# Head sums by ScalarE's accumulator, value blocks added up in PSUM, batch 0 in quarters and joined tails, in a linear-attention and gated-unit kernel

## The chip, the cores and the metric

The kernel runs on one core of one Trainium2 chip. The metric is the device time of one execution in microseconds (us). A core has five engines with a queue of instructions each: TensorE (PE, its weight loads shown apart as PEld), VectorE (DVE), ScalarE (ACT), GpSimd (POOL) and SyncE (SP), which here only starts transfers. They wait for each other by semaphores. The on-chip memory SBUF has 128 partitions; PSUM, into which TensorE writes, has eight banks of 128 x 512 float32.

## The reference

Everything is float32; the weights arrive as float64 and are narrowed on the chip. B = 8 batches, H = 8 heads, S = 576 tokens, D = 64 per head, C = 512 channels.

```python
kv  = np.einsum('bhsd,bhse->bhde', k, v)
out = np.einsum('bhsd,bhde->bhse', q, kv)
rms = np.sqrt(np.mean(out * out, axis=-1, keepdims=True) + 1e-06)
x   = (out / rms * g_norm)               # then (B,H,S,D) -> (B, S, H*D)

xp = np.concatenate([np.zeros((B, 4, C)), x], axis=1)
gate_pre = sum(conv_w[k] * xp[:, k:k + S, :] for k in range(5))
gate = 1.0 / (1.0 + np.exp(-gate_pre))
val  = x @ w_val
result = (gate * val) @ w_out
```

## The kernel before

The work of a batch goes through these steps; their names are those of the functions in the code, and a number behind a name is a batch, a chunk of 128 tokens (four full ones, and the tail, chunk 4, of 64 tokens) or a part.

*Attention.* `kv_product` multiplies k by v for all heads with 64x64 products (L476); `kv_copy` brings the result to SBUF. `turn_q` turns q on VectorE with its 32x32 block transpose (batches 0 and 1: `turn_q_rows` on TensorE, L515, and `sort_q`). `raw_pair` and `raw_tail` (L551) multiply q by kv into PSUM, two chunks or the tail at a time, in two banks (one for each half of the heads). Batch 0 has a form of its own: `kv_half` puts kv of two heads into a block-diagonal 128x128 matrix `kv_bd`, and `raw_half` (L563) uses 128-wide products. Then `square` squares on ScalarE into `sq` (L600; L596 for batch 0), `sums` adds up the 64 squares of each head on VectorE (L607; a 65th column holds the epsilon), `powers` raises the sums to -1/2 on GpSimd (L617), and `normalise` multiplies: on ScalarE in 64-element instructions with a scale for each head (L636), for batch 0 on VectorE (L626).

*Turning x.* The normalised chunk must stand with channels on partitions. Batches 0 and 1, and all tails, do it on TensorE (`turn_x` L648, `keep_x` L655); the others with VectorE's block transpose (`turn_blocks` L661) and transfers that move the blocks (`move_blocks` L669, alternately from SyncE's and GpSimd's queue). `halo` (L676, GpSimd) fills the four columns in front for the convolution.

*Gate.* `gate_start` (ScalarE, L680), four `gate_tap` (VectorE, L686), `gate_end` (sigmoid on ScalarE, L693) for each of four groups of 128 channels.

*Values.* Batches 0 and 1 compute x @ w_val with eight plain products each (`val_product`, L698, and `keep_val`). Batches 2 to 7 use Strassen's scheme in Winograd's form, which needs seven products of half-size blocks where the plain way needs eight: `val_sums` and `x_sums` form sums of weight and x blocks on VectorE, `val_fast` (L747) makes the seven products for each of two column groups `mj`, in three PSUM accumulators a, b, c, and `val_keep` (L754 to L768) brings them out: 0, 1, 2 and 6 are copies on ScalarE, 3, 4 and 5 are additions on VectorE into the value tile `gv`, in SBUF. `gated` multiplies `gv` by the gate (VectorE, L711).

*Output.* For each pair of batches i and each of its four token pairs p, `token_sums` (VectorE, L816), `fast_product` (L838) and `fast_keep` (ScalarE copies, VectorE adds at L848) do the same seven-product scheme with w_out. The two 64-token tails of a pair of batches are done by `out_product i 8`, plainly: for each half, four products with 64 columns of weights and 512 moving columns (L785).

*Weights.* `narrow_weight` turns float64 words into float32 by bit operations in eight passes (n = 0 to 7): 0, 4, 5, 6, 7 on VectorE, 1 to 3 on ScalarE (L405, L407, L409).

What sets the order of everything is one long text, `PLAN`. It lists every step, and each engine's queue gets its instructions in that order. The numbers behind an `@` are the buffers that a step takes, among them the PSUM banks 0 to 7. `start_warm` issues products without use (L464) to keep TensorE at work while it has nothing to do.

Of the kernel before, what the change touches and what calls it, by code (L numbers as in the profile page):

```python
# [9 lines left out]
FP32 = mybir.dt.float32  # L10
# [5 lines left out]
P = 128  # L16
# [3 lines left out]
load_q_rows 0 1; load_q_rows 0 0; load_half v 0 0 @ 0; load_half k 0 0 @ 0; load_half v 0 1 @ 0;  # L20
load_half k 0 1 @ 0; start_warm 5 256 @ 0; warm_up; stage_weight wval 0; stage_weight wval 1;
stage_weight cw 0 @ 0; turn_q_rows 0 4 @ 1; turn_q_rows 0 3 @ 2; sort_q 0 4 @ 0; turn_q_rows 0 0 @ 3;
turn_q_rows 0 2 @ 4; sort_q 0 3; turn_q_rows 0 1 @ 5; start_warm 3 256 @ 6; load_q_rows 1 0; load_q_rows 1 1;
sort_q 0 0; stage_weight wval 2; kv_product 0 0 @ 7 0; narrow_weight cw 0 0 @ 0; load_half k 1 1; sort_q 0 2;
load_half v 1 1; kv_half 0 0; sort_q 0 1; raw_half 0 3 0 @ 1; narrow_weight cw 0 1; narrow_weight cw 0 2;
kv_product 0 1; stage_weight wval 3; narrow_weight cw 0 3; load_half k 1 0; narrow_weight cw 0 4;
narrow_weight cw 0 5 @ 0; raw_half 0 0 0 @ 2; stage_weight wout 1 @ 1; narrow_weight cw 0 6 @ 1; kv_half 0 1;
narrow_weight cw 0 7; narrow_weight wval 0 0 @ 1; raw_half 0 3 1; narrow_weight wval 0 5 @ 2;
narrow_weight wval 0 1; raw_half 0 0 1; narrow_weight wval 0 6 @ 3; turn_cw @ 6; square 0 3 @ 0;
raw_half 0 2 0 @ 3; keep_cw; square 0 0 @ 1; sums 0 3 @ 0 0; raw_half 0 2 1; narrow_weight wval 0 2;  # L30
raw_half 0 4 1 @ 4; sums 0 0; powers 0 3; load_half v 1 0; square 0 2 @ 2; raw_half 0 4 0;
narrow_weight wval 1 0 @ 0; raw_half 0 1 0 @ 5; square 0 4 @ 0; sums 0 2; narrow_weight wval 0 3;
raw_half 0 1 1; sums 0 4; load_half v 2 1 @ 0; start_warm 1 256 @ 0; narrow_weight wval 1 1;
narrow_weight wval 0 4; powers 0 2; square 0 1 @ 1; narrow_weight wval 1 5 @ 0; narrow_weight wval 1 2;
narrow_weight wval 0 7; stage_weight wout 0 @ 2; turn_q_rows 1 3 @ 7; normalise 0 3 @ 0;
narrow_weight wval 1 3; turn_q_rows 1 2 @ 6; sums 0 1; sort_q 1 3 @ 1; turn_q_rows 1 1 @ 0;
load_half v 2 0 @ 0; narrow_weight wval 2 0 @ 1; turn_x 0 3 @ 1; narrow_weight wval 1 6 @ 1; powers 0 1;
normalise 0 4 @ 1; narrow_weight wval 2 1; turn_q_rows 1 0 @ 7; load_q 2 2; normalise 0 2 @ 2; turn_x 0 4 @ 4;
keep_x 0 3; narrow_weight wval 1 4; turn_x 0 2 @ 3; keep_x 0 4; narrow_weight wval 2 2;
narrow_weight wval 2 5 @ 2; kv_product 1 1 @ 1 4; narrow_weight wval 1 7; keep_x 0 2;  # L40
narrow_weight wval 2 6 @ 3; sort_q 1 1; val_product 0 1 1 @ 3; narrow_weight wval 3 0 @ 0;
narrow_weight wval 3 5 @ 0; halo 0; normalise 0 1 @ 0; narrow_weight wval 3 1; normalise 0 0 @ 1;
narrow_weight wval 2 3; narrow_weight wval 3 6 @ 1; turn_x 0 1 @ 0; narrow_weight wval 3 2; turn_x 0 0 @ 5;
narrow_weight wval 2 4; load_half k 2 1 @ 0; val_product 0 0 1 @ 2; keep_x 0 1; narrow_weight wout 1 5 @ 2;
keep_x 0 0; narrow_weight wval 2 7; narrow_weight wval 3 3; narrow_weight wout 1 0 @ 1;
narrow_weight wout 1 6 @ 0; gate_start 0 0 @ 0; kv_product 1 0; narrow_weight wval 3 4; gate_start 0 3 @ 1;
gate_tap 0 0 3; sort_q 1 2; turn_q_rows 1 4 @ 0; narrow_weight wval 3 7; val_product 0 0 0 @ 5; load_q 2 0;
gate_tap 0 0 2; keep_val 0 0 1; gate_tap 0 3 3; gate_start 0 1 @ 2; sort_q 1 4; val_sums 2;
val_product 0 3 0 @ 6; gate_tap 0 1 3; kv_copy 1 1; kv_copy 1 0; load_q 2 1; sort_q 1 0; gate_tap 0 0 1;
raw_tail 1 @ 0 2; gate_tap 0 3 2; raw_pair 1 3 @ 1 4; square 1 4 @ 2; narrow_weight wout 0 5 @ 3;  # L50
keep_val 0 0 0; gate_tap 0 0 0; val_product 0 2 1 @ 7; gate_start 0 2 @ 3; gate_tap 0 3 1; square 1 3 @ 0;
square 1 2 @ 1; sums 1 4 @ 1 1; gate_tap 0 2 3; narrow_weight wout 1 1; powers 1 4; load_half k 2 0 @ 0;
val_product 0 1 0 @ 5; sums 1 3; keep_val 0 1 1; stage_weight wout 3 @ 0; gate_end 0 0; gate_tap 0 1 2;
powers 1 3; narrow_weight wout 1 2; sums 1 2; narrow_weight wout 1 3; val_product 0 2 0 @ 3; gated 0 0;
keep_val 0 3 0; keep_val 0 2 1; gate_tap 0 2 2; normalise 1 4 @ 2; powers 1 2; narrow_weight wout 1 4;
normalise 1 3 @ 0; raw_pair 1 1 @ 7 6; turn_q 2 0 @ 0; stage_weight wout 2 @ 1; turn_q 2 2; turn_x 1 4 @ 0;
load_q 2 3; val_product 0 3 1 @ 2; gate_tap 0 3 0; keep_x 1 4; normalise 1 2 @ 1; gate_tap 0 2 1;
narrow_weight wout 0 6 @ 2; turn_x 1 3 @ 0; keep_val 0 3 1; gate_tap 0 1 1; load_q 3 1; turn_x 1 2 @ 1;
# [172 lines left out]
def kernel(  # L231
# [104 lines left out]
    def head(hp, r):  # L336

        return r * (H // 2) + hp
# [579 lines left out]
```

## Time and profile before

The median of three runs is 295.33 us (295.32 to 295.54). The profiled execution has a span of 294.9 us, from the first to the last instruction; what lies around the span is thus about 0.4 us.

| engine | busy us | share of the span | instructions |
|---|---|---|---|
| PE | 287.0 | 97% | 3279 |
| PEld | 226.9 | 77% | 3279 |
| DVE | 268.7 | 91% | 483 |
| ACT | 198.7 | 67% | 621 |
| POOL | 120.7 | 41% | 131 |

One float32 matmul of the program shows as two rows in the profile. A row's listed duration is from its start to its modelled end, and the next row starts before that end; so the rate at which rows follow each other is read from stretches of the chain, not from the mean duration. Short instructions on ScalarE overlap in the same way. In a line of the groups stand: line of the code, engine, operation, out<-in, shapes, count | busy time of the group in us, mean ns of one instruction | idle time of the engine ahead of them and who ended it.

### The profile page before, as it was taken

The numbers are of one execution on the slowest core, as the hardware profiler recorded it, in microseconds if no ns is written. First come the engines' busy times: TensorE is split into PE (matmuls) and PEld (weight loads), VectorE is DVE, ScalarE is ACT, GpSimd is POOL, SyncE is SP. The second block draws the span as 40 slices with busy tenths as digits, with TensorE's granted clock in tenths as the row PEclk, the third lists the DMA queues.
The fourth block names the chain that finished last, engine by engine and source line by source line (L and its number), as shares of the span: only waits on it lengthen the run. The fifth ranks groups of instructions, "written<-read, shape, count | busy, mean of one in ns | idle before, by whom it ended". The sixth has DMA issues, their size and how long they took to land.

```text
span 294.9 us, 8675 instructions
## 1 busy us (share of the span) xinstructions
PE 287.0 (97%) x3279; PEld 226.9 (77%) x3279; DVE 268.7 (91%) x483; ACT 198.7 (67%) x621; POOL 120.7 (41%) x131
## 2 busy tenths in 40 slices
PE   7999999999999999999999999999999999999994
PEld 3776878788887768878887767888887588788583
DVE  1699999999999999999999999999998999999812
ACT  2899999999786667867477576659588433723330
POOL 3067054854491477421881649021592072000020
PEclk9997999999999999999999999999999999999999
DMA  7999998886686766946789789534553170221344
GB/s 268 379 392 410 284 276 230 239 258 176 197 189 198 234 150 182 341 144 174 182 237 279 167 218 308 165 112 109 141 128 80 44 170 2 57 53 36 98 105 120
DMA packets 32009, 55.51 MB, mean 188 GB/s; under 512 B 6166, under 2 KB 14358, under 8 KB 31968
## 3 DMA queue, kind: packets, MB, share of 16 engines
q1 hardware_dynamic: 29328, 49.50, 57.2%
q0 software_dynamic: 1760, 3.43, 5.2%
q10 hardware_dynamic: 880, 2.03, 1.8%
q8 instruction: 26, 0.43, 0.6%
q14 instruction: 15, 0.12, 0.1%
HBM read 39.21 MB, written 9.44 MB: 165 GB/s over the span
## 4 chain that ended last, share of the span: by engine, by line
PE 94%; DMA 2%; ACT 1%; DVE 1%; issue 0%
PE bank L838 33%; PE bank L747 28%; PE bank L698 11%; PE bank L476 7%; PE bank L551 6%; PE bank L785 5%; PE bank L648 2%; DMA qs<-in_q_dram 2%; PE bank L563 2%; PE bank L515 1%; PE bank L464 0%; ACT wexp L409 0%; DVE x L626 0%; ACT sq L596 0%; DVE ss L607 0%; ACT wexp L407 0%
## 5 line engine op out<-in xcount | busy, mean ns | idle before, releaser
L617 POOL TENSOR_TENSOR rt<-ss,mhalf 128x8 f32<-128x8 f32 (+3 forms) x38 | 73.1, 1937 | 82.0 <-DVE ss L607 81.8
L686 DVE SCALAR_TENSOR_TENSOR gate<-xT,cwT,gate 128x576 f32<-128x576 f32 x128 | 100.4, 807 | 0.2
L636 ACT ACTIVATE x<-bank,rt 128x64 f32<-128x64 f32 x252 | 56.1, 375 | 3.5 <-POOL rt L617 3.2
L838 PE MATMUL bank<-wsum,w 128*128 128x256 f32 x192 | 47.3, 381 | 0.0
L669 POOL DMA_DIRECT2D xT<-y x48 | 26.6, 559 | 41.6 <-DVE gv L754 13.5
L838 PEld LDWEIGHTS bank<-wsum,w 128*128 128x128 f32 x192 | 36.0, 190 | 6.1 <-issue 0.8
L747 PE MATMUL bank<-xs,vsum 128*128 128x288 f32 x144 | 37.1, 407 | 0.0
L747 PEld LDWEIGHTS bank<-xs,vsum 128*128 128x128 f32 x144 | 27.3, 190 | 7.3
L698 PE MATMUL bank<-xT,wval 128*128 128x288 f32 x128 | 32.8, 411 | 0.0
L838 PE MATMUL bank<-wout,gv 128*128 128x256 f32 x128 | 32.3, 382 | 0.0
L698 PEld LDWEIGHTS bank<-xT,wval 128*128 128x128 f32 x128 | 24.0, 192 | 6.3
L693 ACT ACTIVATE gate<-gate 128x576 f32<-128x576 f32 x32 | 23.0, 727 | 7.9 <-DVE gate L686 7.8
L838 PEld LDWEIGHTS bank<-wout,gv 128*128 128x128 f32 x128 | 24.0, 190 | 3.5
L680 ACT ACTIVATE gate<-xT,cwT 128x576 f32<-128x576 f32 x32 | 25.2, 804 | 0.9 <-DVE gv L711 0.9
L747 PE MATMUL bank<-xT,wval 128*128 128x288 f32 x96 | 25.7, 406 | 0.0
L600 ACT ACTIVATE sq<-bank 128x256 f32<-128x256 f32 (+1 forms) x70 | 21.6, 400 | 6.0 <-PE bank L551 5.8
L711 DVE TENSOR_TENSOR gv<-gv,gate 128x576 f32<-128x576 f32 x32 | 23.5, 745 | 2.0 <-ACT gate L693 1.5
L607 DVE TENSOR_REDUCE ss<-sq 128x8 f32<-128x520 f32 (+1 forms) x40 | 24.7, 624 | 0.5 <-ACT sq L600 0.4
L848 DVE TENSOR_TENSOR ot<-bank,ot 128x256 f32<-128x256 f32 (+1 forms) x32 | 17.2, 546 | 8.4 <-PE bank L838 4.1
L747 PEld LDWEIGHTS bank<-xT,wval 128*128 128x128 f32 x96 | 18.2, 190 | 4.5
L854 ACT COPY ot<-bank 128x256 f32<-128x256 f32 x16 | 6.0, 376 | 22.6 <-PE bank L838 22.6
L551 PEld LDWEIGHTS bank<-kv,qT 64*64 64x64 f32 x1008 | 16.3, 135 | 4.8 <-issue 2.1
(91 smaller groups left out, 469.4 us busy)
## 6 DMA issues: line engine op xcount, KB each, us to landing
qs<-in_q_dram SPq DMA_DIRECT2D x96, 140.0 KB, 4.0
out_dram<-ot SPq DMA_DIRECT2D x136, 64.0 KB, 1.7
k<-in_k_dram SPq DMA_DIRECT2D x14, 576.0 KB, 4.9
v<-in_v_dram SPq DMA_DIRECT2D x12, 576.0 KB, 5.3
xT<-y POOLq DMA_DIRECT2D x48, 64.0 KB, 2.7
xT<-y SPq DMA_DIRECT2D x48, 64.0 KB, 2.7
y<-in_moe_w_val_dram SPq DMA_DIRECT2D x4, 512.0 KB, 11.9
w<-in_moe_w_out_dram SPq DMA_DIRECT2D x4, 512.0 KB, 7.1
```

The source lines that it names most:

```text
L551: nc.tensor.matmul(st["raw", b, c][r][cols, to * D:(to + 1) * D], st["qT", b][rows, hp, first:first + D], kvs[b % 2][rows, hp, :], start=T ...
L607: nc.vector.reduce_sum(out=st["ss", b][:, FIRST[c]:FIRST[c] + n], in_=st["sq", b, c][:, 0:n], axis=AX.X)
L617: nc.gpsimd.tensor_tensor(out=st["rt", b][:, which], in0=st["ss", b][:, which], in1=mhalf[:, which], op=ALU.pow)
L636: nc.scalar.activation(out=x[:, to * D:(to + 1) * D], in_=raw[:, h * D:(h + 1) * D], func=AF.Copy, scale=root[:, to:to + 1])
L669: (nc.sync if i % 2 else nc.gpsimd).dma_start(out=xTs[b % 2][i * TB:(i + 1) * TB, :, first:first + P], in_=y[a * TB:(a + 1) * TB, i])
L680: nc.scalar.activation(out=gate[:], in_=xTs[b % 2][:, jt, HALO:SX], func=AF.Copy, scale=cwT[:, K - 1, jt:jt + 1])
L686: nc.vector.scalar_tensor_tensor(out=gate[:], in0=xTs[b % 2][:, jt, tap * TB:tap * TB + S], scalar=cwT[:, tap, jt:jt + 1], in1=gate[:], op ...
L693: nc.scalar.activation(out=gate[:], in_=gate[:], func=AF.Sigmoid)
L698: nc.tensor.matmul(val[:], wval[:, kc, jt * P:(jt + 1) * P], xTs[b % 2][:, kc, HALO + n * SV:HALO + (n + 1) * SV], start=(kc == 0), stop=( ...
L711: nc.vector.tensor_tensor(out=both, in0=both, in1=st["gate", b, jt][:], op=ALU.mult)
L747: nc.tensor.matmul(st[bank, "val", b, mj][:], weights_[:, k], tokens()[:, k], start=(n in (0, 1, 3) and k == 0), stop=(k == NK // 2 - 1), ...
L838: nc.tensor.matmul(st[bank, i, p], tokens()[:, k], weights_[:, k], start=(n < 2 and k == 0), stop=(k == NK // 2 - 1), skip_group_check=True)
```

## The change

1. *Head sums.* For batches 1 to 7, `square` writes each head's 64 squares to a tile `junk` that nobody reads and has ScalarE's accumulator add them up into one column of `ss`: 252 instructions of 64 elements in place of 70 of 128 or 256. `sums` on VectorE goes for these batches. GpSimd adds the epsilon to the sums in an instruction ahead of the power.
2. *Value blocks on copied sums.* For all 12 value groups (batches 2 to 7, two each), `val_keep 0` copies accumulator a not to `gv` but to another PSUM bank; the product n = 3 then accumulates onto that copy, and `val_keep 3` is a ScalarE copy where it was a VectorE addition.
3. *Batch 0 in units on quarters.* `kv_bd` and `raw_half` go. `raw_unit g i` makes the 64x64 products of four heads (i) and two chunks (g); `square_unit`, `sums_unit`, `powers_unit`, `normalise_unit`, `turn_unit` and `keep_unit` follow in the same units. Batch 0's value products come in two parts, one for each i. So that the halves of the seven-product scheme fall together with the units, its channel blocks are now the even and the odd ones (`EARLY`, `LATE`).
4. *Four batches' tails joined.* `keep_tail` gathers the 64 tail tokens of two batches into 128 columns; two such pairs are the two token blocks of one more seven-product output, i = 4 for batches 0 to 3 and i = 5 for batches 4 to 7. The plain `out_product` is no longer used.
5. *Engines chosen in the order.* A last argument 1 on some steps puts a copy or a pass on VectorE instead of ScalarE (`copy`): among them `normalise 1 1`, `normalise 2 3`, `gate_start 1 2` and six output copies. Pass 2 of `narrow_weight` now clamps and scales in one VectorE instruction; pass 3 goes.
6. *The order.* `PLAN` is written anew, with other banks; `move_blocks` has two steps now, one with SyncE's two transfers and one with GpSimd's two.

```diff
 PLAN = """
...
-raw_tail 3 @ 3 4; kv_product 4 0; val_keep 2 1 6; gated 1 2; square 3 4 @ 0; turn_blocks 3 2;
-out_product 0 8 @ 1; sums 3 4; kv_copy 4 1; kv_copy 4 0; turn_blocks 3 3; val_keep 2 0 6; powers 3 4;
...
+narrow_weight cw 0 7; turn_cw @ 5; keep_cw; narrow_weight wval 0 0 @ 1; square_unit 0 0 @ 0; sums_unit 0 0 @ 0 0;
...
+val_keep 2 0 0 @ 0; store 0 0; val_fast 2 1 2; val_keep 2 1 2; powers 3 4; normalise 3 4 @ 2; load_half v 5 0 @ 0;
...
+fast_product 5 0 0 @ 2; fast_keep 5 0 0 1 @ 2; fast_product 3 1 3; fast_keep 3 1 5; fast_product 5 0 2;
...
-    ACT_SUMS = ()
+    ACT_SUMS = (1, 2, 3, 4, 5, 6, 7)
+    SEEDED_OUT = set()
+    SEEDED_VAL = {(4, 0), (7, 1), (2, 1), (3, 1), (6, 1), (7, 0), (2, 0), (5, 1), (3, 0), (5, 0), (6, 0), (4, 1)}
...
+    junk = const.tile([P, H // 2, D], FP32, name="junk")
+    EARLY, LATE = slice(0, NK, 2), slice(1, NK, 2)
...
+    def copy(e, out, in_):
+        if e:
+            nc.vector.tensor_copy(out=out, in_=in_)
+        else:
+            nc.scalar.copy(out=out, in_=in_)
...
         elif n == 2:
-            nc.scalar.activation(out=e, in_=e, func=AF.Relu, bias=biases[0:rows, 1:2], scale=-1.0)
-        elif n == 3:
-            nc.scalar.activation(
-                out=e, in_=e, func=AF.Identity, bias=biases[0:rows, 2:3], scale=-float(1 << 23))
+            nc.vector.tensor_scalar(
+                out=e, in0=e, scalar1=MOST, scalar2=float(1 << 23), op0=ALU.min, op1=ALU.mult)
...
     def square(b, c):
         n = heads(c)
-        sq = st["sq", b, c] = new("sq", [P, H, D + 1], FP32, f"sq{b}_{c}")
         if b in ACT_SUMS:
             new_sums(b)
+            first = columns(b, c).start
             for r, raw in enumerate(st["raw", b, c]):
                 for h in range(n // 2):
                     to = r * n // 2 + h
                     nc.scalar.activation(
-                        out=sq[:, to, 0:D], in_=raw[:, h * D:(h + 1) * D], func=AF.Square,
-                        accum_out=st["ss", b][:, FIRST[c] + to:FIRST[c] + to + 1])
-            return
...
+                        out=junk[:, h], in_=raw[:, h * D:(h + 1) * D], func=AF.Square,
+                        accum_out=st["ss", b][:, first + to:first + to + 1])
             return
...
+    def root(b, which):
+        ss, rt = st["ss", b][:, which], st["rt", b][:, which]
+        if b in ACT_SUMS:
+            nc.gpsimd.tensor_scalar_add(ss, ss, D * EPS)
+        nc.gpsimd.tensor_tensor(out=rt, in0=ss, in1=mhalf[:, which], op=ALU.pow)
...
+    def raw_unit(g, i):
+        if ("unit", i) not in st:
+            st["unit", i] = [ps([P, 2, 4, D], f"unit{i}_{r}") for r in range(2)]
+        st["unit", g, i] = banks = [bank[:, g].rearrange("p (j m) e -> p j m e", j=2) for bank in st["unit", i]]
+        for m in range(2):
+            for j, c in enumerate(UNIT[g]):
+                for half in range(2):
+                    for r in range(2):
+                        rows, cols = slice(r * D, (r + 1) * D), slice(half * D, (half + 1) * D)
+                        first = c * P + half * D
+                        nc.tensor.matmul(
+                            banks[r][cols, j, m, :], st["qT", 0][rows, 2 * i + m, first:first + D],
+                            kvs[0][rows, 2 * i + m, :], start=True, stop=True)
...
+        begins = (0, 1) if (b, mj) in SEEDED_VAL else (0, 1, 3)
+        if n in begins:
             st[bank, "val", b, mj] = ps([P, SV], f"v{bank}{b}_{mj}")
         for k in range(NK // 2):
             nc.tensor.matmul(
                 st[bank, "val", b, mj][:], weights_[:, k], tokens()[:, k],
-                start=(n in (0, 1, 3) and k == 0), stop=(k == NK // 2 - 1), skip_group_check=True)
+                start=(n in begins and k == 0), stop=(k == NK // 2 - 1), skip_group_check=True)
...
+        if seeded and n == 0:
+            st["b", "val", b, mj] = ps([P, SV], f"seed{b}_{mj}")
...
         if n == 0:
-            nc.scalar.copy(out=to(0, 0), in_=a)
+            copy(on, out=b_ if seeded else to(0, 0), in_=a)
...
+        elif n == 3 and seeded:
+            copy(on, out=to(0, 0), in_=b_)
...
+    def keep_tail(b, on=0):
+        if ("tail", b // 2) not in st:
+            st["tail", b // 2] = new("sq", [P, NK, P], FP32, f"tail{b // 2}")
+        first = b % GVS * S + SF
+        copy(
+            on, out=st["tail", b // 2][:, :, b % 2 * T:(b % 2 + 1) * T], in_=gv[:, :, first:first + T])
...
-        chunk = lambda r, k: lambda: gv[:, k, begin + r * P:begin + (r + 1) * P]
+        chunk = lambda r, k: lambda: (
+            gv[:, k, begin + r * P:begin + (r + 1) * P] if i < B // 2 else st["tail", 2 * (i - B // 2) + r][:, k])
```

In the changed kernel's profile the head sums stand at L584, the added constants at L602 and the powers at L603, the chunk normalise at L621 (ScalarE) and L614 (VectorE), batch 0's units at L641 to L683, the value products at L734 and L783, the output products at L898; all copies stand at L336 (VectorE) or L338 (ScalarE).

More of the change, by code (lines that the diff above doesn't have):

```diff
@@ L30 @@
[L30 to L35, printed above, removed]
@@ L830, in fast_product @@
             ("a", chunk(1, ODD), wsum[:, 3]))[n]
+        if (i, p) in SEEDED_OUT:
+            if n == 0:
+                both = ps([P, 2, C // 2], f"ac{i}_{p}")
+                st["a", i, p], st["c", i, p] = both[:, 0], both[:, 1]
+            for k in range(NK // 2):
+                nc.tensor.matmul(
+                    st[bank, i, p], tokens()[:, k], weights_[:, k],
+                    start=(n == 0 and k == 0), stop=(k == NK // 2 - 1), skip_group_check=True)
+            return
         if bank == "a" and n == 0:
@@ L859, in fast_keep @@
         else:
[L860 to L861 removed]
+            copy(on, out=second[:, LOW], in_=a)
     def store_last(i, c, n):
```

669 lines of the change are left out of this document (342 added, 327 removed).

## The prediction

> **What bounds the kernel now.** I read the busy shares first, then the chain that ended last, then both in stretches, and last the groups of the lines that the change touches.
>
> ```profile
> PE 287.0 (97%) x3279; PEld 226.9 (77%) x3279; DVE 268.7 (91%) x483; ACT 198.7 (67%) x621; POOL 120.7 (41%) x131
> ...
> PE 94%; DMA 2%; ACT 1%; DVE 1%; issue 0%
> ```
>
> The chain, in order of time (start, length, what ran):
>
> ```profile
> 14.08 1.91 PE bank L563 x12
> 16.16 1.72 PE bank L563 x16
> ...
> 27.04 2.47 PE bank L698 x8
> ...
> 58.14 2.02 PE bank L551 x128
> ...
> 91.14 10.87 PE bank L747 x44
> ...
> 276.38 3.58 PE bank L785 x16
> 279.96 10.57 PE bank L838 x48
> ```
>
> Length over count is what a matmul row costs on this path, below its listed duration because rows overlap: L838 0.216 us (0.220 in this piece), L747 and L698 0.243, L785 0.224, L551 and L476 0.016, L563 0.107, the turns through L515 and L648 0.105. Times their counts (448, 336 + 128, 64, 1008 + 1152, 36, 84) that is 270 us of matmul work. The last matmul ends at 290.5, so 20 us went to waiting and warm-up; about 14.5 us of work lie in the first 30 us, so 15.5 of the 20 were lost there, 4.5 later. The last copy and its stores take 4.4 more.
>
> ```profile
> 15.00:30.00 15.00, 13.61 (x146) 10.70 (x146) 14.80 (x32) 13.65 (x29) 9.98 (x7) 0.89 1.04 400
> 30.00:45.00 15.00, 15.00 (x206) 11.58 (x204) 14.49 (x24) 14.80 (x41) 4.61 (x3) 1.00 0.98 270
> 45.00:60.00 15.00, 15.00 (x383) 12.68 (x382) 15.00 (x30) 14.97 (x56) 8.55 (x7) 1.00 0.86 236
> 60.00:250.00 190.00, 190.00 (x2192) 151.78 (x2185) 187.51 (x321) 131.30 (x440) 93.16 (x102) 1.00 0.64 177
> ```
>
> After the stretch the columns are its length, then PE, PEld, DVE, ACT, POOL. VectorE is full beside TensorE from 15 to 250 us; ScalarE is full only up to 60 us, then 69%.
>
> ```profile
> L636 ACT ACTIVATE x<-bank,rt 128x64 f32<-128x64 f32 x252 | 56.1, 375 | 3.5 <-POOL rt L617 3.2 <-DVE y L661 0.3
> L607 DVE TENSOR_REDUCE ss<-sq 128x8 f32<-128x520 f32 x32 | 21.6, 679 | 0.1
> L600 ACT ACTIVATE sq<-bank 128x256 f32<-128x256 f32 x56 | 18.3, 424 | 3.5 <-PE bank L551 3.3
> L754 DVE TENSOR_TENSOR gv<-bank,gv 128x288 f32<-128x288 f32 x36 | 15.8, 443 | 0.8 <-PE bank L747 0.8
> L785 PE MATMUL bank<-wout,gv 128*64 128x512 f32 x64 | 14.6, 598 | 0.0
> L600 ACT ACTIVATE sq<-bank 128x128 f32<-128x128 f32 x14 | 3.3, 302 | 2.5 <-PE bank L551 2.5
> L332 ACT ACTIVATE warm<-warm 128x1 f32<-128x1 f32 x1 | 0.2, 203 | 0.0
> ```
>
> **The change part by part.**
> *Tails.* L785 goes: 64 rows x 0.224 = 14.3 us. Two tail products of seven terms come, 14 program matmuls each, two rows per matmul: 56 rows x 0.216 = 12.1. All on the path: -2.2 us. Their sums, copies and adds lie on VectorE and ScalarE (below).
>
> *Batch 0 by quarters.* The 40 rows of L563 (4 half wide) cost about 3.9 us; 144 rows of 64x64 cost 144 x 0.016 = 2.3: -1.6, in the start. The value products come in parts, but are the same 128 rows. Heads now pass in two groups, so the first group can be squared after half of k and v, where before the first square (15.8 us) stood behind both. That could bring the first L698 (27.04) forward by up to 4 us; but its weights are narrowed on VectorE, full from 15 us on. SyncE's loads come in another order, the last two w_val tiles and batch 1's k and v later, with the 16 DMA engines full either way (400 GB/s in the second stretch); and the granted clock was 0.89 in that stretch, which another pattern of gaps can better or worsen by up to 1.6 us. I take -1, ends -4 and +3 (the halves wait for one another). Six more warm-up matmuls stand in gaps where TensorE waits anyway; if one is late it costs 2 x 0.22 us.
>
> *VectorE.* Away: all 40 sums 24.8 us; 12 adds x 0.443 = 5.3; batch 0's normalising 3.0; four sorting copies 1.7; a memset 0.5. Added: 5 sums of batch 0, 3.1; its normalising in 8 pieces x 0.416, 3.3; chunks 1 1 and 2 3 normalised here, 1.7; the clamp that replaces L407 and L409, 8 x 0.43 + 0.2 = 3.6; tail sums 8 x 0.41, and adds 2.2, together 5.5; six copies, 2.6; a gate start and small ones, 0.9. Net 268.7 - 14.6 = 254. It is hidden work, but its relief is what lets TensorE keep its pace where the two are level.
>
> *ScalarE, without the head sums.* Away: L600 21.6, L407 and L409 12.8, batch 0's squares 2.7, kvbd copies 1.7, tail copies 2.4, moved to VectorE 5.9. Added: batch 0's squares 3.9, tail gathering 8 x 0.4 = 3.2, 12 block copies x 0.41 = 4.9, tail keeps 2.3, sorting 1.1. 198.7 - 47.1 + 15.4 = 167.
>
> *The head sums.* 252 squares of 64 elements with an accumulated output come. No row shows one. Plain, such a square is 302 - (424 - 302) / 2 = 241 ns long, and rows below start 0.13 to 0.16 us before the one ahead ends, say 0.12: 0.12 us each, the low end. High end: the accumulator is read by an instruction of its own, not shorter than the one-element row (203 ns), nothing overlapping: 0.44. I take 0.20, from the nearest shape: the 252 normalising instructions have the same 64 elements, the same banks and one operand more than a plain one, and eight start within 1.57 us:
>
> ```profile
> 101.67 1.73 ACT L636 ACTIVATE x<-bank,rt 128x64 f32<-128x64 f32 x8
> 103.24 0.45 ACT L768 COPY gv<-bank 128x288 f32<-128x288 f32 x1
> 103.56 0.48 ACT L600 ACTIVATE sq<-bank 128x128 f32<-128x128 f32 x2
> ```
>
> That is 50 us (30 to 111): ScalarE at 217 us (197 to 278). It must be looked at by stage. In the new order, the steps from behind batch 3's last normalise (3 4) to batch 5's (5 4) hold, on TensorE, 24 value products of four rows (23.3), 20 output products of four (17.3), k-v and raw products (9.0) and turns (0.4): 50.0 us. On ScalarE they hold, each instruction less that 0.12, 72 head sums (14.4 at 0.20), 64 normalises (12.8), 16 gate passes (10.4) and 36 copies (9.6): 47.2 us. The two are level at 0.24. Up to there ScalarE is covered by TensorE; above it each 0.01 us costs 0.36 us a batch, 2.5 us over seven batches. Behind the squares on ScalarE's queue stand the copies that free the banks, so TensorE would wait for those. For being so nearly level I add 1 us.
>
> *Powers.* GpSimd gets 35 small adds ahead of L617; between its memsets (0.10 us) and the halo copy (0.57): 4 to 20 us on an engine at 41% that waits for sums (81.8 us). The chain to the normalise grows by that 0.1 to 0.6, but loses the reduction (0.68). Nothing on the path.
>
> *Seeds.* In all 12 value groups a copy from bank to bank replaces the copy to SBUF, and the fourth product accumulates onto it. TensorE now waits for that copy (0.41 us), with the whole of its queue behind; products of other groups stand in between, so 0, at worst 12 x 0.4 = 5.
>
> *Queues.* The block moves are split between SyncE and GpSimd, same 96 in number; four stores go from GpSimd to SyncE: 0.5 us of issue each, not at the end. The end (copy, halved stores) is as before: 4.4 us.
>
> Sum: the span of the profiled run is 294.9 and the median 295.33, 0.43 more. 294.9 - 2.2 - 1.6 - 1 + 1 = 291.1 span, 291.5 as a median.
>
> **A rule against it.** The Trainium skill (VectorE: DVE Perf Modes, section "Two Vector instructions with no wait between them") says that a Vector operation that writes out its accumulator is two instructions, the operation and an accumulator read. It says nothing of ScalarE, and no row here shows either. Carried over to ScalarE, the rule would make the first rival's time, about 304, of this sum.
>
> **The rivals.**
> *ScalarE becomes the bound* (the other side). Place: the head sums of batches 1 to 7. Decisive point: with 3.8 us to lose, 0.24 + 3.8 / 252 = 0.255 us per sum. With a 203 ns read that overlaps by the usual 0.12 for both, a sum is 0.20; with the read waiting for the square, 0.32 (241 + 203 - 120): 252 x 0.08 = 20 us above level, of which batches 6 and 7 can hide a third behind the late output products, so +13: 304. For it: ScalarE is nearly level even at 0.20. Against: the 64-element rows pipeline well. 27%.
> *The start gets longer.* Batch 1's value products wait for batch 1's normalising, now behind more squares, and taps of batch 0 crowd there on VectorE: +6 of the 15.5 us already lost: 297.5. For it: all engines full to 60 us. Against: the same work in all. 8%.
> *Only the matmuls count.* The relief of VectorE and the halves bring nothing: 294.9 - 2.2 with batch 0's 1.6 hidden, plus the level engines' 1: 293.7 to 294.9 as a median. 14%; a quarter of it within 0.2%.
> *The start gains its 4 us* and the 4.5 us lost later halve: 294.9 - 3.8 - 4 - 2 = 285.1, with seeds at half their worst 287.6; 288 as a median. 10%.
>
> **Numbers.** The forecast case, 290 to 293.2, has 41%. Range 287.5 to 303: it leaves out the worse half of the first rival (14%) and a little below. Own range of the likeliest: 290 to 293. 0.2% (0.6 us) is about what a measurement here can tell from no change. Faster: 41 + 10 + 10 = 61%; same 4%; slower 27 + 8 = 35%.
>
> **What would show it.** L898 with 504 rows at 0.216 us; no L785; VectorE near 254 and ScalarE near 217 busy, starts 0.20 us apart within eight head sums; first L734 before 27 us; PE still over 95% of the chain. Wrong, if head sums start 0.26 us or more apart and TensorE's waits name ScalarE, or if the chain before 60 us names VectorE or ScalarE for longer than now.

## The result, and the profile after

The changed kernel takes 313.54 us (median of 4 runs, 311.5 to 316.7) against 295.32 for the kernel before (295.0 to 295.5): a ratio of 1.060, 95% interval 1.056 to 1.063. It is 18.2 us slower, where 291.5 was forecast. Medians here and below are of all executions, ratios and their intervals of those within 1.5% of the fastest of their kernel. The profiled execution of the changed kernel is the longest of its four, 316.7 us, and its granted clock is low behind its waits; places are read from it, totals from the medians.

The page of the changed kernel: busy time by engine, and the chain that ended last by engine.

```profile
PE 291.1 (92%) x3387; PEld 234.2 (74%) x3387; DVE 256.5 (81%) x466; ACT 220.8 (70%) x1045; POOL 124.8 (40%) x164
...
PE 73%; DMA 8%; ACT 5%; SPq 4%; issue 4%; DVE 3%; POOL 2%; DVEq 0%; POOLq 0%; ACTq 0%
```

VectorE (256.5) and ScalarE (220.8) came out as forecast (254 and 217). But TensorE holds 73% of the chain, where it had 94%, and transfers, SyncE's queue and "issue" have taken its place.

A ledger says where. For every TensorE row of the two traces, take the time to the start of the next row and subtract the usual pitch of its shape (0.243 us for 288 columns, 0.216 for 256, 0.211 for the 512-column rows of L785, 0.1065 for 128, 0.0148 for 64x64). What is left is lost time; warm-up rows and the few rows of other shapes count as lost whole. In us:

| stretch of the span, us | before | after |
|---|---|---|
| 0 to 30 | 14.8 | 14.8 |
| 30 to 50 | 1.1 | 6.8 |
| 50 to 90 | 1.7 | 1.7 |
| 90 to 130 | 0.9 | 12.4 |
| 130 to 150 | 0.7 | 5.0 |
| 150 to the end | 2.6 | 2.9 |
| lost in all | 21.8 | 43.6 |
| rows at their usual pitch | 267.3 | 264.7 |

The matmul work fell by 2.6 us. Three places lose 21.5 us more: 5.7 at 30 to 50, 11.5 at 90 to 130, 4.3 at 130 to 150. From 150 us on, and from 50 to 90, TensorE loses what it lost before. Behind TensorE's last row the end takes 0.7 us longer (5.4 us from its start to the end of the span, 4.7 before).

Not all of the 21.5 us is standing still. Each place has a stretch in which the granted clock is half, and TensorE's rows are slower there (stretch, length, busy time of TensorE, weight loads, VectorE, ScalarE and GpSimd with counts, granted clock, share of the transfer engines, GB/s):

```profile
40.70:44.10 3.40, 3.28 (x27) 2.57 (x28) 3.40 (x6) 1.86 (x17) 0.43 (x1) 0.50 1.05 304
122.60:129.50 6.90, 6.10 (x15) 4.89 (x16) 6.90 (x13) 0.60 (x3) 2.62 (x3) 0.51 1.04 252
146.50:149.90 3.40, 3.40 (x9) 2.45 (x8) 2.98 (x5) 2.46 (x18) 2.48 (x5) 0.50 0.77 180
```

Rows in these stretches lose 1.8, 3.1 and 1.7 us by the ledger, 6.6 in all. The kernel before has one such stretch while it works, from 24.3 to 27.7 us.

*First place, 30 to 50 us.* The chain of waits of the changed kernel, each line with its start, its length and what it was:

```profile
36.02 0.44 ACT kv L338 x2
36.46 0.04 issue
36.50 1.14 PE bank L551 x58
37.65 3.18 issue
40.82 0.91 PE bank L551 x22
```

L551 is batch 1's raw product: 16 rows of the tail, then 64 of the pair. TensorE stops after 42 of those 64, between rows that read the same tiles, and stands for 3.2 us, waiting for nothing that the profile shows.

*Second place, 90 to 130 us.* The list of TensorE's waits (us in total, times, longest), then SyncE's and VectorE's timelines (start, length, line, operation, tiles, count, and in brackets the idle time before and what ended it):

```profile
PE bank L898 <- DVE w L866: 6.2, 1, 6.2
PE bank L551 <- issue: 4.2, 2, 3.2
PE bank L783 <- issue: 2.4, 2, 2.2
```

```profile
105.03 0.46 SPq L348 DMA_DIRECT2D k<-in_k_dram  x1
105.54 5.37 SPq L939 DMA_DIRECT2D out_dram<-ot  x4
111.02 6.24 SPq L701 DMA_DIRECT2D xT<-y  x8
117.36 10.39 SPq L358 DMA_DIRECT2D qs<-in_q_dram  x20
```

```profile
113.60 0.46 DVE L793 TENSOR_TENSOR gv<-bank,gv 128x288 f32<-128x288 f32 x1 [0.25 <-PE bank L783]
121.84 0.71 DVE L498 STREAM_TRANSPOSE qT<-qs 128x512 f32<-128x512 f32 x1 [7.79 <-DMA qs<-in_q_dram]
122.60 0.65 DVE L866 TENSOR_TENSOR w<-gv 128x512 f32<-128x512 f32 x1
```

VectorE comes to the turn of batch 5's query pair 2 at 114.1 and stands 7.8 us, since the load leaves SyncE only at 117.4: between it and the query load ahead (95.0 to 98.1) the queue holds two key and two value loads, twelve stores and eight block moves. The token sums (L866) are queued behind the turn, and TensorE's output products (L898) behind the sums. In the kernel before, the same load leaves SyncE at the same time, but its turn runs at 131.7 us (a line of SyncE's timeline and one of VectorE's):

```profile
117.39 2.97 SPq L358 DMA_DIRECT2D qs<-in_q_dram  x4
131.66 0.69 DVE L500 STREAM_TRANSPOSE qT<-qs 128x512 f32<-128x512 f32 x1
```

The new order brings the turn 18 us forward and leaves the load where it was. The chain, whose releasers are inferred, follows SyncE's block moves back to the landing of a key load.

```profile
105.03 9.04 DMA k<-in_k_dram
114.09 0.58 SPq L701
```

Key loads take 9.1 us to land at the median, 4.9 in the kernel before.

*Third place, 143 us:* 2.2 us of "issue" again, ahead of a value product (L783). A shorter stop of the kind, 1.0 us at 108 us ahead of L551, falls into the second place.

The head sums, on the other hand, cost what was forecast. ScalarE's timeline:

```profile
108.93 0.20 ACT L584 ACTIVATE junk<-bank 128x64 f32<-128x64 f32 x1
109.04 0.19 ACT L584 ACTIVATION_READ_ACCUMULATOR junk<-bank 128x1 f32 x1
109.13 0.21 ACT L584 ACTIVATE junk<-bank 128x64 f32<-128x64 f32 x1
```

A square and its accumulator read start 0.20 us after the pair ahead. The accumulator is a second instruction, as the Trainium skill says of the Vector engine (VectorE: DVE Perf Modes, section "Two Vector instructions with no wait between them"); these rows show the same on ScalarE.

### The profile page after: what moved, and what is told of

It reads as the page before. It is cut to its first block, busy times and chain, and to the rows that moved or that the text cites. A ratio compares the mean times of both kernels' runs of the same rounds, so it can differ in the third digit from the quotient of the medians.

```text
span 314.9 us, 9334 instructions
## 1 busy us (share of the span) xinstructions
PE 291.1 (92%) x3387; PEld 234.2 (74%) x3387; DVE 256.5 (81%) x466; ACT 220.8 (70%) x1045; POOL 124.8 (40%) x164
## 4 chain that ended last, share of the span: by engine, by line
PE 73%; DMA 8%; ACT 5%; SPq 4%; issue 4%; DVE 3%; POOL 2%; DVEq 0%; POOLq 0%; ACTq 0%
PE bank L898 31%; PE bank L783 21%; PE bank L734 8%; PE bank L551 5%; PE bank L478 3%; DMA k<-in_k_dram 3%; ACT qT L338 3%; DMA qs<-in_q_dram 2%; SPq L358 2%; PE bank L466 2%; DMA v<-in_v_dram 2%; POOL rt L603 1%; PE bank L513 1%; PE bank L683 1%; SPq L701 1%
## 5 line engine op out<-in xcount | busy, mean ns | idle before, releaser
L603 POOL TENSOR_TENSOR rt<-ss,mhalf 128x8 f32<-128x8 f32 (+1 forms) x40 | 71.0, 1776 | 15.4 <-DVE ss L654 12.5
L898 PE MATMUL bank<-wsum,w 128*128 128x256 f32 x216 | 54.9, 393 | 6.2 <-DVE w L866 6.2
L584 ACT ACTIVATE junk<-bank 128x64 f32<-128x64 f32 x252 | 54.7, 318 | 7.4 <-PE bank L551 7.4
L621 ACT ACTIVATE x<-bank,rt 128x64 f32<-128x64 f32 x240 | 54.7, 422 | 2.8 <-POOL rt L603 2.8
L584 ACT ACTIVATION_READ_ACCUMULATOR junk<-bank 128x1 f32 x252 | 53.9, 303 | 0.0
L898 PEld LDWEIGHTS bank<-wsum,w 128*128 128x128 f32 x216 | 41.9, 197 | 13.8 <-ACT x L621 6.5
L338 ACT COPY ot<-bank 128x256 f32<-128x256 f32 x65 | 26.8, 438 | 31.7 <-PE bank L898 29.1
L338 ACT COPY gv<-bank 128x288 f32<-128x288 f32 x64 | 28.6, 458 | 23.0 <-PE bank L783 22.4
L783 PE MATMUL bank<-xs,vsum 128*128 128x288 f32 x144 | 40.1, 414 | 2.2 <-issue 2.2
L602 POOL TENSOR_SCALAR ss<-ss 128x8 f32<-128x8 f32 (+1 forms) x35 | 14.2, 407 | 61.9 <-ACT junk L584 60.8
L701 POOL DMA_DIRECT2D xT<-y x48 | 26.7, 563 | 24.4 <-PE bank L783 9.9
L734 PE MATMUL bank<-xT,wval 128*128 128x288 f32 x128 | 35.2, 421 | 0.5 <-issue 0.3
L783 PEld LDWEIGHTS bank<-xs,vsum 128*128 128x128 f32 x144 | 27.6, 194 | 10.2 <-issue 2.6
L911 DVE TENSOR_TENSOR ot<-bank,ot 128x256 f32<-128x256 f32 (+1 forms) x36 | 19.8, 551 | 16.2 <-PE bank L898 12.4
L898 PE MATMUL bank<-wout,gv 128*128 128x256 f32 x128 | 32.6, 380 | 0.0
L734 PEld LDWEIGHTS bank<-xT,wval 128*128 128x128 f32 x128 | 24.1, 196 | 7.2 <-ACT qT L338 0.6
L783 PE MATMUL bank<-xT,wval 128*128 128x288 f32 x96 | 28.2, 421 | 0.8 <-ACT kv L338 0.4
L898 PEld LDWEIGHTS bank<-wout,gv 128*128 128x128 f32 x128 | 24.2, 190 | 3.9
L716 ACT ACTIVATE gate<-xT,cwT 128x576 f32<-128x576 f32 x31 | 24.9, 830 | 1.3 <-DMA qs<-in_q_dram 1.1
L498 DVE STREAM_TRANSPOSE qT<-qs 128x512 f32<-128x512 f32 x24 | 16.8, 699 | 9.5 <-DMA qs<-in_q_dram 9.5
L551 PEld LDWEIGHTS bank<-kv,qT 64*64 64x64 f32 x1024 | 17.2, 136 | 9.0 <-issue 6.9
```

Source lines behind the costliest of these rows:

```text
L338: nc.scalar.copy(out=out, in_=in_)
L551: nc.tensor.matmul(st["raw", b, c][r][cols, to * D:(to + 1) * D], st["qT", b][rows, hp, first:first + D], kvs[b % 2][rows, hp, :], start=T ...
L584: nc.scalar.activation(out=junk[:, h], in_=raw[:, h * D:(h + 1) * D], func=AF.Square, accum_out=st["ss", b][:, first + to:first + to + 1])
L603: nc.gpsimd.tensor_tensor(out=rt, in0=ss, in1=mhalf[:, which], op=ALU.pow)
L621: nc.scalar.activation(out=x[:, to * D:(to + 1) * D], in_=raw[:, h * D:(h + 1) * D], func=AF.Copy, scale=roots[:, to:to + 1])
L701: (nc.gpsimd if e else nc.sync).dma_start(out=xTs[b % 2][i * TB:(i + 1) * TB, :, first:first + P], in_=y[a * TB:(a + 1) * TB, i])
```

## The experiments

Theory Q: the new order asks for transfers when the queue and the transfer engines cannot give them. Theory A, the first rival of the prediction: ScalarE with its head sums is what TensorE waits for. Each run is compared with the kernel before on the same chip (295.3 to 295.6 us); "loses" is the ledger's figure.

### The head sums: put in alone, in part, taken out, thinned

The kernel before with the accumulator alone, GpSimd's 35 small adds included (each batch's first square also takes the sums' buffers):

```diff
-    ACT_SUMS = ()
+    ACT_SUMS = (1, 2, 3, 4, 5, 6, 7)
-... sums b c ...                     (35 steps, batches 1 to 7)
```

> The kernel before with the head sums of batches 1 to 7 by ScalarE's accumulator alone: 35 reductions leave VectorE (22 us), ScalarE gets 252 pairs at 0.195 us in place of 70 squares (about +27 us, to 226). Theory Q (the accumulator is cheap enough, the loss is in the new order of the loads): 293 to 296 us. Theory A: 300 us or more, with TensorE's waits on ScalarE.

317.0 us (316.9 to 318.4; ratio 1.073, 1.069 to 1.077). Theory Q's forecast for this run was wrong by 21 us. The page's chain by engine, the longest of TensorE's waits, and ScalarE's timeline where the first of them is:

```profile
PE 54%; ACT 29%; DVE 6%; DMA 4%; issue 2%; POOL 1%; SPq 1%; DVEq 0%; ACTq 0%
```

```profile
PE bank L698 <- ACT xT L655: 2.9, 2, 2.3
PE bank L838 <- ACT ot L850: 2.2, 2, 1.9
PE bank L747 <- ACT gv L758: 1.5, 2, 1.3
```

```profile
63.56 0.88 ACT L409 ACTIVATE wexp<-wexp,biases 128x512 uint32<-128x512 uint32 x1
64.17 0.38 ACT L591 ACTIVATE sq<-bank 128x64 f32<-128x64 f32 x1
...
67.22 0.49 ACT L591 ACTIVATION_READ_ACCUMULATOR sq<-bank 128x1 f32 x1
67.31 1.37 ACT L655 ACTIVATE xT<-bank 128x512 f32<-128x512 f32 x2
```

Sixteen pairs stand for 3.1 us in front of the copy of x^T (L655) that TensorE's value products (L698) need. ScalarE is busy 229.8 of 316.7 us, far from full, and yet holds 29% of the chain: in an order made for squares of 0.4 us, what counts is the copy behind them, not the sum.

The same for batches 3 to 7 only, `ACT_SUMS = (3, 4, 5, 6, 7)`:

> The kernel before with the accumulator for batches 3 to 7 alone; batches 1 and 2, whose work lies beside the weights' conversion on ScalarE, keep their reductions. Theory E (the 21 us that the accumulator cost in the old order came from the stage up to 110 us, where ScalarE is full): 296 to 301 us. If the accumulator costs the same in every batch: 15 us more than before, 310.

307.3 us (306.4 to 308.3; ratio 1.041, 1.037 to 1.044): 12.0 us for five batches, 2.4 each, which leaves 9.4 for the two early ones. The full early stage costs more, but the accumulator is dear in that order everywhere.

The reverse, the changed kernel with the reductions back:

```diff
-    ACT_SUMS = (1, 2, 3, 4, 5, 6, 7)
+    ACT_SUMS = ()
+... square b c @ sq; sums b c ...    (35 steps)
```

> The changed kernel with the accumulator alone undone: batches 1 to 7 are squared in 70 halves on ScalarE again and summed by 35 reductions on VectorE, in the place where the head sums stood. ScalarE falls by about 27 us to 193, VectorE rises by about 22 us to 278. Theory Q (the loads' order costs the time; in the new order VectorE has no room): 316 to 328 us, slower than the change. Theory A (the head sums on ScalarE are what made the change slow, in this order too): below 306 us.

338.8 us (337.4 to 339.7): 25 us slower than the change, and more than either theory said. TensorE loses 11.6 us at 50 to 90 (1.7 in the change) and 14.2 after 200 (1.4). Removing the accumulator does not undo the loss. The 25 us are the price of reductions in this place: each stands right behind its square, with two of four buffers in turn (one buffer more than the change has), and VectorE stands 19.7 us for squares. Another place for them was not tried.

The changed kernel with a quarter of the pairs:

```diff
-                for h in range(n // 2):
-                    ... square one head, accumulate
+                ... square a half (4 heads) at once, accumulate once
```

> The changed kernel with one squared and accumulated instruction per half (256 elements) in place of four of 64, so a quarter of the 252 pairs; three of four head sums are left out and the values are not the reference's. ScalarE falls by some 20 to 25 us, all else stays. Theory A (ScalarE's head sums hold TensorE, by their place in its queue if not by their sum): 305 us or less. Theory Q (they do not, but for a little at the start): 311 to 314 us.

311.8 us (308.0 to 313.8), with ScalarE at 200 us. Three of four head sums are left out; 20 us less work on ScalarE bring 1.8 us of the 18.2, and the ranges overlap. In the new order theory A falls.

### The query loads: one ahead, all ahead, some ahead

```diff
+load_q 5 2;
 move_blocks 3 0 0; move_blocks 3 2 0; gate_end 1 1; move_blocks 3 1 0; ...
-load_q 5 2;
```

> The changed kernel with one query load, that of batch 5, pair 2, moved ahead of six block moves on SyncE's queue; every other engine's order is untouched. Theory Q (the in-order SyncE queue held that load until 117.4 us, VectorE waited 7.8 us for it and TensorE 6.2 us behind VectorE): about 307 us (305 to 309), TensorE's 6.2 us wait for the token sums gone. Theory A (ScalarE with its head sums is the bound): 313 us, no change, a wait of the same size elsewhere. Theory D (the transfers themselves are full in that stretch): 311 to 314, the load lands as late as before.

308.8 us (307.0 to 312.1), 4.7 less than the change, from a single step on one queue: the loss at 90 to 130 goes from 12.4 to 6.3 us. The next query loads are late in turn (VectorE waits three times, 5.0 us).

```diff
 turn_q b h;
+load_q (the next load into that buffer);   (for all 24)
```

> The changed kernel with all query loads of batches 2 to 7 placed right behind the turn that frees their buffer, so ahead of block moves, stores and key and value loads. Theory Q: all 10.7 us lost between 90 and 130 us come back, and those at 140 to 150 do not: about 303 us (301 to 306). Theory A: 313. Theory D: 309 to 314, since the key and value loads land later in exchange.

322.3 us (320.4 to 324.5), where theory Q said 303. The 90 to 130 us stretch loses only 1.3, but 30 to 50 loses 12.5 and 50 to 90 8.8. SyncE, in order, now stands from 10.2 to 24.4 us at the first hoisted load until batch 1's turns free its buffer, with batch 1's keys and values behind it. TensorE's longest wait in this run (us in total, times, longest):

```profile
PE bank L478 <- DMA gv<-in_v_dram: 8.8, 1, 8.8
```

So query loads were moved past block moves and stores only, never past a key or value load:

> The changed kernel with query loads moved ahead of block moves and stores only, never ahead of a key or value load, and two of batch 2 ahead of the output-weight load for which SyncE stood from 32.2 to 38.8 us. Theory Q: the 10.7 us lost between 90 and 130 us shrink to 3 or less without the losses that the earlier placing of all loads made between 30 and 80 us: 304 to 307 us. Theory A: 309 or more.

310.2 us (309.0 to 311.1). 90 to 130 falls to 6.2. Half of the forecast: the loads are issued earlier and still land late.

### Other ways to move the same wait

Turns of batch 5's pairs 2 and 3 some 50 steps later on VectorE, with the loads that need their buffers:

> The changed kernel with the turns of batch 5's query pairs 2 and 3 moved some 50 steps later on VectorE (still ahead of batch 5's raw products), and the two query loads that follow those turns moved with them. No load is hastened. Theory Q (VectorE, in order, stands in front of a turn whose load is late, with the token sums queued behind it): TensorE's 6.2 us wait goes, 305 to 308 us. If the token sums were late for another reason: 311 or more.

321.0 us (319.0 to 322.6). Wrong, and telling. 90 to 130 loses 7.0 instead of 12.4, but 150 to 200 now 14.4 instead of 1.5: a late turn frees its buffer late, so batch 6's load is late. VectorE's longest wait here:

```profile
DVE qT L498 <- DMA qs<-in_q_dram: 14.9, 2, 11.4
```

Load, turn and next load form one chain through three buffers; nothing was gained here by delaying a link. Batch 5's key and value loads behind the query loads:

> The changed kernel with batch 5's four key and value loads (576 KB each, 98 to 105 us, up to 9 us to land) moved behind the query loads of pairs 2 and 3. Theory D (these transfers, asked for early, fill the engines and the queue ahead of the late query load): 306 to 309 us. If they only moved the wait: a wait of the key-value products for them at 125 to 135 us, 313 or more.

314.1 us (312.6 to 317.1), no gain: TensorE waits 3.9 us in front of key-value products at 124 us (the profile names the landing of a query load, which these products do not read), and 150 to 200 loses 7.2. The late turns, the sorting copies below and the one load ahead, together:

> The changed kernel with the late turns, the sorting copies on VectorE and batch 5's query load of pair 2 ahead of six block moves. Theory Q with theory S: 8 to 10 us of the 18.2 come back, 303 to 306 us; what is left are the two instruction stalls and a start that is 2 to 3 us longer.

321.1 us (320.8 to 322.2) instead of 303 to 306: with the late turns it is as slow as they are alone, and 150 to 200 loses 14.0.

### The transfers left out

```diff
     def load_q(b, hp):
         t = qs[:, (b * HP + hp + 1) % 3]
+        if b > 2:
+            st["q", b, hp] = t
+            return
```

> The changed kernel without the query loads of batches 3 to 7 (80 of 96 transfers of 140 KB; the turns read what stands in the buffers, so the values of these batches are not the reference's). Theory Q (a chain of query load, turn, next load through three buffers and SyncE's queue sets TensorE's waits from 90 to 150 us): the 10.7 us go and the time is 300 to 304 us. Theory A (ScalarE's head sums): 311 or more.

```diff
-        t = qs[:, (b * HP + hp + 1) % 3]
+        t = qs[:, 1 + hp % 2 if b > 2 else (b * HP + hp + 1) % 3]
...
-        st["q", b, hp] = t
+        st["q", b, hp] = qs[:, 0] if b > 2 else t
```

> The same, but with all 80 transfers made, into two buffers that nobody reads: the queue and the transfer engines carry what they did, only no turn waits for a load and no load for a turn (the values of batches 3 to 7 are not the reference's). If the waits between loads and turns are the price: as without the loads, 300 to 305 us. If the price is the room that these transfers take on the queue and the transfer engines, so that others are late: 308 or more.

307.4 us (305.6 to 309.3) without the loads, 309.6 (306.0 to 312.2) with them made but awaited by nobody. The ledger reads 2.7 and 4.3 us at 90 to 130. So the price there is for the most part the waiting of turns for loads, some 4 to 6 us in the medians, less than the 10 forecast. The two ranges overlap, so what the transfers cost by their room alone stays open.

### The start: ScalarE or the instructions

Sorting copies of batch 1 earlier on ScalarE, and, in another run, on VectorE:

```diff
 sort_q 1 2;
+sort_q 1 1; sort_q 1 3;
```

> The changed kernel with two groups of sorting copies of batch 1 (chunks 1 and 3, eight copies on ScalarE) moved ahead of gate starts and value copies on ScalarE. Theory S (batch 1's raw products were late at 30 to 37 us because these copies stood behind other work on ScalarE): TensorE loses 2 to 3 us less between 30 and 50 us: 310.5 to 311.5. If only the 3.2 us stall without a visible cause matters there: 313 to 314.

```diff
-sort_q 1 1; sort_q 1 3;
+sort_q 1 1 1; sort_q 1 3 1;
```

> The changed kernel with the eight sorting copies of batch 1's chunks 1 and 3 on VectorE instead of ScalarE, in their place. Theory S (ScalarE, full from 27 to 37 us, holds batch 1's raw products): 2 to 3 us of the 6 lost between 30 and 50 us come back: 310.5 to 311.5 us. If the instruction stall alone counts there: 313 to 314.

313.6 us (309.8 to 317.6) and 312.1 (311.0 to 314.6). Neither can be told from the change: the first loses 3.2 us less at 30 to 50 and 2.8 more before 30, the second 6.4 against 6.8 at 30 to 50. With the query load ahead as well:

> The changed kernel with the two edits that each gained alone: batch 5's query load of pair 2 ahead of six block moves (308.8 us) and eight sorting copies on VectorE (312.1). If the gains add: 307 to 308 us. If a gain at 30 to 50 us is lost again where the next query load is late: 308.5 to 309.5.

310.8 us (309.2 to 311.9): nothing adds up. ScalarE's copies are not the start's loss.

The stall without a cause, with rows added ahead of it:

```diff
-start_warm 3 256 @ 3;
+start_warm 30 16 @ 3;
```

> The changed kernel with 3 warm-up products of 256 columns at the start replaced by 30 of 16 columns: 54 more TensorE rows before the first query turn, nothing else moved. Theory F (the two TensorE stalls without a visible cause, before its 604th and 2127th rows, are blocks of instructions that arrive late): the stalls stand before the same counts of rows, so 54 rows earlier in the work, or vanish. If they come from something that this point of the work waits for, they stand before the rows 658 and 2181.

319.9 us in a single execution. In the change TensorE stands, put down to "issue", ahead of its 604th row (3.4 us from start to start), its 1748th (1.3) and its 2127th (2.6). With 54 rows more it stands ahead of its 604th (1.2) and 2127th (0.9) again, which are now other pieces of work, and also ahead of the 859th (2.0), the 1114th (2.9), the 1621st (1.3), the 2381st (1.6) and the 2759th (1.4). All lie multiples of some 127 rows apart (255, 507, 378 and so on), and each row is a weight load and a matmul: some 254 instructions. That is the grain of the instruction queue. The page's queues for the changed kernel (packets, megabytes, share):

```profile
q8 instruction: 26, 0.43, 0.6%
```

26 packets of 16 KB for 2 x 3387 instructions of TensorE: one packet for each 260 or so. In the trace of the change one of them runs from 38.3 to 39.5 us, inside the stall (37.6 to 40.8), and the one ahead of it at 31.1, when the transfer engines were full. Is that why it is late?

```diff
+        if b == 2: st["q", b, hp] = qs[:, 0]; return         (load_q)
-        ... dma_start(out=t, in_=src)                        (load_half)
+        if b not in (2, 3): ... dma_start(out=t, in_=src)
```

> The changed kernel without batch 2's query loads and without the key and value loads of batches 2 and 3 (which are asked for between 22 and 60 us), so that the transfer engines, at a share of 1.04 from 28 to 38 us, have little to do there; the values of these batches are not the reference's. Theory F1 (the instruction block that TensorE waits for before its 604th row is late because these transfers fill the engines): the 3.2 us stall at 37.6 us goes or falls under 1.5 us. Theory F2 (it is asked for late, whatever the transfers do): it stays at 3 us.

306.0 us (304.2 and 307.9). The windows of the change and of this run (stretch, length, busy time of TensorE, weight loads, VectorE, ScalarE and GpSimd with counts, granted clock, share of the transfer engines, GB/s), then this run's chain:

```profile
28.00:38.00 10.00, 9.04 (x226) 7.02 (x224) 8.38 (x17) 9.89 (x30) 0.76 (x3) 1.00 1.04 361
38.00:48.00 10.00, 7.18 (x44) 5.41 (x44) 10.00 (x18) 5.53 (x42) 5.80 (x6) 0.83 0.70 194
```

```profile
28.00:38.00 10.00, 9.07 (x249) 7.26 (x247) 8.30 (x17) 9.89 (x29) 0.76 (x3) 1.00 0.22 86
38.00:48.00 10.00, 9.38 (x233) 7.62 (x234) 10.00 (x18) 9.82 (x74) 7.96 (x8) 1.00 0.61 170
```

```profile
36.59 1.41 PE bank L555 x80
38.00 4.08 PE bank L738 x16
```

With the engines at 0.22 instead of 1.04, the 80 rows (L555 is the change's L551) run in one piece; the packet starts at 34.1 us instead of 38.3. ScalarE is as full as before (9.89 of 10 us), and TensorE loses 3.3 us at 30 to 50 instead of 6.8. The loads of batches 2 and 3 made this block of instructions late. Of the 3.3 us, 1.2 are a stop at 47.4 us ahead of the 859th row, so the next blocks still come late. The stop ahead of the 2127th row falls from 2.6 to 0.8 us here, though these loads are long over by then; without the query loads of batches 3 to 7 it stays at 2.4. Why is not shown. The kernel, now ahead, meets the late query load harder (7.7 us at 111).

### Both omissions at once

> The changed kernel without any query load of batches 2 to 7 and without the key and value loads of batches 2 and 3: the two omissions joined (the values of batches 2 to 7 are not the reference's). If late transfers, by instruction blocks at the start and by query loads later, are what keeps the change from the sum of its matmul work, the gains add: 296 to 300 us, with 2 us lost at 30 to 50 and 3 at 120 to 140. If the engines themselves fall behind each other in the new order: 303 or more.

299.0 us (297.8 to 300.3; ratio 1.012, 1.007 to 1.016). Its chain by engine:

```profile
PE 78%; ACT 8%; POOL 5%; DMA 3%; DVE 2%; issue 2%; SPq 0%; ACTq 0%; DVEq 0%; POOLq 0%
```

The gains add (6.1 and 7.5 us apart, 14.5 together): 14.5 of the 18.2 us hang on transfers, queries and the early keys and values. That is what leaving them out is worth, so about the most that better times for them could bring. The same omissions were not tried in the kernel before; its ledger leaves them little to win, 4.4 us from 30 to 150 us. The other 3.6 stay: TensorE loses 25.9 us against 21.8 before, 1.2 more at 30 to 50, 2.5 more at 90 to 130 (there the chain runs through ScalarE's squares, two powers of 2.1 us on GpSimd and ScalarE's normalising) and 1.1 more after 200, and the 2.6 us of matmul work do not pay for it. With the end, 0.7 us longer, that makes the 2.3 us between the two traces (297.2 and 294.9). The rest is between traces and medians: in this run 1.9 us lie around the span, and in the experiments as much lies around that of the kernel before (295.4 against 293.6), not 0.4; so its trace of 294.9 is likely of an execution some 1.3 us longer than its median. Even with these transfers free the change is not faster; none of these runs points to a version that beats the kernel before.

## Why the prediction was wrong

- *Queues* was the step that failed: "0.5 us of issue each, not at the end". It counted the block moves and stores but not the loads that share SyncE's queue with them. It was written that the load order of the start is another; that every query turn of batches 4 and 5 comes earlier, by up to 25 us, was not looked at. Batch 5's pair 2 is the one that broke: its load leaves at 117.4 us in both kernels, its turn is reached at 114 instead of 132. Costed at nothing; 6.1 us go when the query loads of batches 3 to 7 are taken out, 14.5 with the early loads too. No rival had it either.
- *Batch 0 by quarters*, the start: -1, ends -4 and +3. Up to 30 us nothing was won or lost (14.8 both; the first value product is 2.1 us earlier, 24.9 against 27.0). The loss came behind it, +5.7 at 30 to 50, outside the bounds. The rival "the start gets longer" (+6, 297.5) had place and size, but not the cause: it named batch 1's normalising behind squares and taps; for the most part it was an instruction block behind loads (3.4 us) and the slower rows behind the stop (1.8). "The 16 DMA engines full either way" was read off the profile rightly and was the warning: what else needs them was not asked.
- *The head sums*: 0.20 us each, measured 0.20; ScalarE 217, measured 221. The price was right. The point that the two are level at 0.24 and ScalarE is covered up to there was not a safe rule: in the old order the same 0.20 costs 21 us, because the copies behind the squares come later, though ScalarE idles 87 us. The step itself said that those copies stand there. In the new order the sums are covered but for 1.8 us or so, which is near the +1 set for it. The same price was covered in one order and not in the other; the sum of the work did not tell them apart.
- *ScalarE becomes the bound* (304): the side was right, the mechanism not, in this order: a quarter of the pairs brings 1.8 us. The read is an instruction of its own, as this rival had it, but the pairs start every 0.20 us, not the 0.255 or more that it needed. A sign of being wrong was seen: the chain does run through ScalarE from 24.2 to 36.5 us (turned chunks, sorting copies, gate starts, a weight pass), but TensorE, with other work in between, stands less than 1 us for it, and moving eight of the sorting copies did not clearly shorten the time.
- *Tails* and the quarters' rows: -2.2 and -1.6 forecast, -2.6 together in the ledger. L785 was priced at 0.224 a row; its rows run at 0.211.
- *VectorE* (254, measured 256.5) was right as a sum. Its relief does not show in the time, since TensorE was the bound; with the reductions back in their squares' places this order takes 25 us more, which is their place as well as their 19 us of work.
- *Seeds* at nothing: none of TensorE's long waits names a copy into a bank; the shorter ones that do are at most 0.45 us long in any run. Not tried alone.
- *Powers* at nothing: GpSimd's small adds take 0.41 us each (14.2 us); in the last run two powers lie on the chain for 4 us, so a part of the remaining 3.6 us may be theirs. Not settled.
- *The end* was to be as before; it takes 0.7 us more.

## What to carry to other kernels

When an order changes, read when each load is wanted and how long ahead it is issued, queue by queue, before costing any engine; a kernel whose engines all get lighter can still be starved by a load that stands behind eight block moves. Full transfer engines delayed more than the data here: where TensorE ran short rows, its own instructions, which come through them too, were late. An instruction's price says little without what stands behind it on its queue: the same 0.20 us pairs cost 21 us in the old order, while in the new one leaving three of four out brought 2. And a stop can cost more than its length: here a third of the loss was slower rows, at a granted clock of 0.50, at the end of the stops and behind them.

## What the runs showed that was not expected

- Instruction blocks of TensorE can be late by 3 us. The Trainium skill (Runtime: NRT & Kernel Launch, section "Instruction fetch mechanics") has the sequencer fetch blocks of 256 instructions by a transfer queue of its own, mostly hidden. The 16 KB packets agree. Hidden they were in the kernel before, where no wait of TensorE is put down to "issue"; in the change, with the engines at a share of 1.04 and some 200 rows of 64x64 at 0.0148 us each just ahead, one stall took 3.2 us.
- Placing every load as early as its buffer allows made the kernel slower by 9 us than the change (322.3 against 313.5): in an in-order queue an early load that must wait for its buffer holds all behind it.
- Gaps were followed by a lower granted clock: 0.66 from 124 to 132 us of the change, right behind the 6.2 us wait, where the stretches without such waits read 1.00. That the gaps caused it was not tried; with both sets of loads left out the clock stays at 1.00 from 6 us to 296.
